# P times V of some key tiles as three f16 products: an attention and gated-linear kernel on one Trainium2 core

## The chip, the core and the metric

The kernel runs on one core of a Trainium2 chip. Its engines work in parallel, each on its own instructions and strictly in their order: PE (TensorE) multiplies matrices into PSUM, ACT (ScalarE) applies functions, DVE (VectorE) and Pool (GpSimd) work on elements, and SP (SyncE) starts the transfers (DMAs). They wait for each other by semaphores. The metric is the device time of one execution in microseconds (us). Before the change it is 1651.75 us, the median of three runs (1650.93 to 1652.77).

## The reference, cut to what matters

```python
B, S, D, H = 1, 2048, 512, 32           # 32 heads of 16, one shared key and value head; F = 1792
mod = (silu(c) @ w_mod).reshape(1, 6, 1, -1)
sa, ca, ga, sb, cb, gb = ...            # six rows of mod
h = layernorm(x) * (1 + ca) + sa
q, k, v = h @ wq, h @ wk, h @ wv        # q in 32 heads, k and v in one
p = softmax(q @ k.T * 16 ** -0.5)       # per head, 2048 x 2048
x = x + ga * ((p @ v) @ wo)             # heads side by side
h = layernorm(x) * (1 + cb) + sb
x = x + gb * (((h @ w_gate) * (h @ w_up)) @ w_down)
```

All inputs and the output are f32.

## The kernel before, in words

**Units and turns.** The attention is cut into 32 units (`u`). Unit u has the 256 queries of block `sb = u // 4` and the 8 heads of group `ch = u % 4`. The loop at L1328 goes through the units, and in each through 16 key tiles of 128 keys (`kt`). One key tile of one unit is a turn; `attend` (L1247) writes out two turns. Two points of a turn will be named often: its middle, and `end_turn` at its end.

In a turn, `qk_exp` (L652) is called four times. Each call makes scores of 128 keys by 512 columns (two heads of 256 queries) on PE and has ACT take their exponential into an f32 tile `P` of 128x512. The row maximum is already in the scores: q carries rows with the negative maximum, and 50 rows take part in the product. The maxima of the next unit are made at the same time: each turn holds four products `mx` (L605) that DVE reduces (L609). At the end of the turn, `pv` (L669) multiplies the P tiles of the turn before with the values: four f32 matmuls at L674, one for each P tile, each with the same 32 columns of `vst` (16 of v, 16 of ones, whose product is the sum of the softmax) and each writing its own 32 partitions of one PSUM bank over all 16 key tiles of the unit. So the four stand in four column strips of PE, and use all its 128 rows.

**Side work.** Between these, each turn has eight places for the other matmuls (the `x` in the string `MANY`, L62): the projection of q, the output projection `wo_work`, gate and up (`gu`), and down. They are f16 products with halves: a factor is split into a high and a low f16 half, and three products (high-high, low-high, high-low, `TERMS`) stand for the f32 one. They use 64 rows of PE each and run beside a score or maximum product on the other 64. They are taken in order from the queue `fill`; a group of gate and up takes 24 places, which is three turns. `half` (L527) makes a group that goes over from one half of the rows to the other wait for an exponential of the turn before (`sync`).

At step 20 of every fourth unit (two steps to a turn) `hooks` (L1307) puts the output projection of the block just done into `fill`, behind what runs and at most one more group, and behind it the rest, with the new block's gate, up and down at the end.

**After a group.** A finished gate and up group is evicted at the end of its turn: ACT and DVE multiply (L868, L870), Pool splits the product into the two f16 halves of `glu` (L871, L872). `glu` has two places, one for blocks with even number and one for odd.

When the second of the two output projection groups (t = 1) is evicted, L755 adds into x, and `after` (L722) puts the rest on ticks. A tick is a call of `drain_posts` (L1148), at the start and in the middle of every turn; in the middle it comes ahead of `hooks`. Counted from that eviction, the statistics come at tick 3 (L762) and tick 4 (L765, then the reciprocal root on Pool, L213 to L218), and the normalisation of the block's two row tiles, `nrm` (L771), at ticks 4 and 9 (L793). For blocks 2 to 5 all of `nrm` is on Pool: L774, L780, L781, L783, L784, each 128x512; for block 6 ACT does the first. Then SP turns the result over by a transposing DMA (L807), four ticks after `nrm`.

**The end of a unit.** The last `pv` of unit u stands at the end of turn 0 of unit u+1, and `pv_out` (L677) at the end of turn 1: ACT copies the bank with a scale `evs`, SP stores it. `normalise` (L685) then follows in four parts at steps 5, 12, 15 and 19 (`NORM_AT`): SP loads the sums and the products, DVE takes the reciprocal, SP spreads it, and Pool multiplies and splits into `och` (L710 to L713), the last of these at the end of turn 9.

SP's queue also carries, in program order, the loads of q for later units (L570) and the rows with the maximum (L643).

Of the kernel before, what the change touches and what calls it, by code (L numbers as in the profile page):

```python
# [39 lines left out]
LATE_Q = 3  # L40
NORM_AT = (5, 12, 15, 19)
NBANK = 8
# [7 lines left out]
PAIRED = 14  # L50
Q_BURSTS = {26: 3, 27: 3, 28: 3, 29: 3}

LOW = -3.0e38
# [12 lines left out]
def adaln_mqa_glu_kernel(ctx: ExitStack, tc: tile.TileContext, x_in, wq_in, wk_in, wv_in, wo_in,  # L66
# [82 lines left out]
    for i in range(3):  # L149
        t = consts.tile([128, 2, 2, ST], F16, name=f"sst{i}")  # L150
        if i == 2:
            nc.gpsimd.memset(t, 0.0)
        sst.append(t)
# [5 lines left out]
    nc.gpsimd.memset(onec, 1.0)  # L159
    ones = consts.tile([128, 128], F32, name="ones")  # L160
# [13 lines left out]
    def marks():  # L174
        lo2 = ident.rearrange("p (a r) -> p a r", a=2)
        for col, r0, r1 in ((0, 16, 32), (1, 32, 48), (2, 48, 50)):
# [122 lines left out]
    def q_evac(u, p):  # L299
        split_rows(sst[u][:, :, p, :], pks[u, p], qsc, sck[:, 3:4], 0.0)  # L300
        ps_give(pks[u, p])
# [16 lines left out]
    def v_mm(b):  # L318
        p = ps_hold("pvt", (128, 4, 16))
        for i in range(4):  # L320
            nc.tensor.matmul(p[:, i, :], parts[b][:, i * 128:(i + 1) * 128], lane[:, 16:32], start=True, stop=True)  # L321

        def out():
            nc.scalar.activation(vst[:, 4 * b:4 * b + 4, 0:16], p, AF.Copy, scale=inv[:, 0:1] if b else 1.0)
            ps_give(p)
        posts.append(out)
# [48 lines left out]
    kb = consts.tile([128, 8], F32, name="kb")  # L375
    inv = consts.tile([128, 3], F32, name="inv")
    fwd = consts.tile([128, 3], F32, name="fwd")
    nc.vector.tensor_copy(kb[:, 0:4], pb[:, 0:4])
# [23 lines left out]
    ln_norm(1, (None, nc.scalar, None, nc.scalar))  # L402
    evs = consts.tile([128, 1], F32, name="evs")

    def ev_scales():

        t = work.tile([128, 2], F32, name="evt", bufs=1)
        nc.vector.tensor_reduce(evs, ident.rearrange("p (a r) -> p a r", a=4)[:, :, 0:16], axis=AX.XY, op=OP.add)
        nc.vector.reciprocal(t[:, 0:1], kb[:, 5:6])
        nc.gpsimd.tensor_tensor(t[:, 0:1], t[:, 0:1], evs, op=OP.mult)  # L410
        nc.gpsimd.tensor_scalar(t[:, 1:2], evs, -1.0, 1.0, op0=OP.mult, op1=OP.add)
        nc.gpsimd.tensor_tensor(evs, t[:, 0:1], t[:, 1:2], op=OP.add)

    qvs = consts.tile([128, 1], F32, name="qvs")
# [42 lines left out]
    def last_rows():  # L457
        wmb = big.tile([128, KC, 1536], F32, name="wmB", tag="wu")
        nc.sync.dma_start(wmb, wm_v[:, :, 1536:3072])
        wmB.append(wmb)  # L460

    wmB = []
    KA, KB = (0, 1), (2, 3)
# [3 lines left out]
    first = {0: lambda: (combine((0, 1), selq), ln_tr(1), ln_stats(6)),  # L467
             1: lambda: (q_evac(0, 1), v_mm(0), ln_norm(2, (VE, SA, VE, SA)), ln_stats(7),
                         q_part(1, 0), q_part(1, 1)),
# [8 lines left out]
             12: lambda: (k_evac(3), h_halves(3, KA)), 13: lambda: h_halves(3, KB),  # L478
             15: lambda: h_halves(1, KA), 17: lambda: h_halves(1, KB), 20: ev_scales}
    later_h = deque((2, k) for k in range(KC))  # L480
# [4 lines left out]
    ended = []  # L485
    sync = {"due": False, "exp": None, "before": None}
    pending = []

    def flush():
        for f in pending:  # L490
            f()
            sync["due"] = True
        pending.clear()

    class Group:
# [31 lines left out]
        def half(self, r):  # L527

            mm = self.put(r, r + 1)
            if self.rows not in (None, r):  # L530
                tc.add_manual_dep(mm.ins, sync["before"], SYNC)
            self.rows, self.turn, sync["due"] = r, now[0], True
            if self.ended():
                ended.append(self)
# [114 lines left out]
    och = {}  # L649
    pd = {}  # L650

    def qk_exp(u, kt, p, a, last=False):  # L652
        s = sst[u % 3]
        ptl[u, kt, p, a] = work.tile([128, D], F32, name="P", tag="P", bufs=8)
        t = ps_sc()
        keys = kst[64 * a:64 * a + 50, kt * 128:(kt + 1) * 128]
        if pending and last:
            for c in range(2):
                if c:
                    flush()  # L660
                nc.tensor.matmul(t[:, c * ST:(c + 1) * ST], keys, s[64 * a:64 * a + 50, c, p, :], start=True, stop=True)  # L661
        else:
            nc.tensor.matmul(t.rearrange("k (c n) -> k c n", c=2), keys, s[64 * a:64 * a + 50, :, p, :],  # L663
                             start=True, stop=True)
        ex = nc.scalar.activation(ptl[u, kt, p, a], t, AF.Exp)  # L665
        if sync["due"]:
            sync.update(due=False, exp=ex.ins.name)

    def pv(u, kt):  # L669
        if kt == 0:  # L670
            pvb[u] = ps_hold("pv")
        for j in range(4):
            p, a = divmod(j, 2)
            nc.tensor.matmul(pvb[u][32 * j:32 * j + 32, :], vst[:, kt, :], ptl[u, kt, p, a],  # L674
                             start=(kt == 0), stop=(kt == KT - 1))

    def pv_out(u):  # L677
        sb, ch = divmod(u, NC)
        ev = work.tile([128, BT], F32, name="ev", tag="ev", bufs=3)
        nc.scalar.activation(ev, pvb[u], AF.Copy, scale=evs)  # L680
        ps_give(pvb[u])
        pd[u] = dram.tile([128, BT], F32, name=f"pd{u}")
        nc.sync.dma_start(pd[u], ev)
# [127 lines left out]
    def ln2_work(sb):  # L811
        st = {}

        def tr(i):
            def f():
                if not h2s:
                    h2T = big.tile([128, 2, 2, KC, ST], F16, name="h2T", tag="wq")
                    glus.append(big.tile([128, 2, 2, FT, ST], F16, name="glu", tag="big"))
# [34 lines left out]
    def ffn_work(sb):  # L853

        def glu():
            return glus[0][:, sb % 2]

# [374 lines left out]
    def side_half(r, cur=cur):  # L1232
# [11 lines left out]
        if cur[0].did[r] < cur[0].n:  # L1244
            cur[0].half(r)

    def attend(u, kt):  # L1247

# [9 lines left out]
        def end_turn(kt):  # L1258
            for g in ended:
                g.finish()  # L1260
            ended.clear()
            for f in ends:
# [12 lines left out]

        for turn in range(2):
            now[0] = u * NSTEP + 2 * (kt + turn)
            sync["before"] = sync["exp"]
            drain_posts()
# [27 lines left out]
    def hooks(u, i):  # L1307
# [4 lines left out]
        side_step(step)  # L1312
        if u > 0 and i in NORM_AT:
            if i == NORM_AT[0]:
                nrm[:] = normalise(u - 1)
            nrm[NORM_AT.index(i)]()
        if i == 20 and u > 0 and u % NC == 0:
            sb = u // NC - 1
# [23 lines left out]

    pv(u, KT - 1)
    pv_out(u)
    sync["before"] = sync["exp"]
# [60 lines left out]
```

## Time and profile before

| | |
|---|---|
| median of three runs | 1651.75 us |
| the profiled execution | 1650.64 us |
| its span, first to last instruction | 1648.9 us |
| PE busy | 1630.6 us, 99% |
| DVE busy | 1401.6 us, 85% |
| ACT busy | 1224.0 us, 74% |
| Pool busy | 554.8 us, 34% |
| clock granted to PE, mean | 0.997 |

The profile comes from one execution. Busy time is the union of an engine's instructions. Matmuls overlap, and their ends are modelled, so for PE the distance from one start to the next says more than a duration. In a line of the timeline the first number is the start in us from the span's start, the second how long the merged instructions took, then come engine, source line, operation, output and inputs, shapes and the count; a bracket tells of idle time of that engine just before, and what ended it. Line numbers are those of the kernel before.

### The profile page before, as it was taken

What the parts mean: (1) busy time and instruction counts of PE and PEld (TensorE: products, weight loads), DVE (VectorE), ACT (ScalarE), POOL (GpSimd) and SP (SyncE); (2) the same over time, 40 slices, a digit from 0 to 9 for tenths busy, and PEclk for the clock granted to TensorE, in tenths of its full rate; (3) what the DMA queues carried; (4) which work ended last, traced back from release to release, by engine and by line L of the source; (5) the groups of instructions that cost most, each with busy time, mean ns of one, the idle gap of its engine ahead of it and who ended that gap; (6) DMA issues with size and microseconds to landing.
All of it is one profiled execution on the core that took longest, in us unless ns stands there. A gap on an engine that the chain in (4) does not pass through costs nothing.

```text
span 1648.9 us, 39747 instructions
## 1 busy us (share of the span) xinstructions
PE 1630.6 (99%) x15629; PEld 743.0 (45%) x15629; DVE 1401.6 (85%) x2434; ACT 1224.0 (74%) x2365; POOL 554.8 (34%) x859
## 2 busy tenths in 40 slices
PE   8999999999999999999999999999999999999998
PEld 4333333355533554335543455434545345444776
DVE  7999999899999999999999999999999999980211
ACT  6688888888877787778877787777778777877300
POOL 5856637864842111401113011400114001410322
PEclk9999999999999999999999999999999999999999
DMA  7213313342211001100001000100001000100100
GB/s 259 97 55 101 94 54 121 91 136 81 78 50 37 20 12 31 38 26 20 20 28 35 26 17 20 39 26 26 20 28 29 26 23 20 39 15 21 33 14 13
DMA packets 78987, 79.05 MB, mean 48 GB/s; under 512 B 30408, under 2 KB 59340, under 8 KB 78800
## 3 DMA queue, kind: packets, MB, share of 16 engines
q1 hardware_dynamic: 77744, 76.46, 15.2%
q8 instruction: 122, 2.00, 0.5%
q14 instruction: 65, 0.53, 0.1%
q10 hardware_dynamic: 1056, 0.07, 0.0%
HBM read 56.04 MB, written 17.05 MB: 44 GB/s over the span
## 4 chain that ended last, share of the span: by engine, by line
PE 94%; ACT 2%; DVE 1%; DMA 1%; issue 1%; POOL 0%; ACTq 0%; SPq 0%
PE side L515 42%; PE pv L674 30%; PE mx L605 8%; PE sc L663 8%; PE sc L661 3%; ACT P L665 1%; DVE mpart L609 1%; DMA xbig<-in_A_x_dram 1%; PE part L283 0%; PE sc L605 0%; PE mxt L633 0%; PE pk L291 0%; DMA wkv<-in_A_wv_dram 0%; DMA sst<-qd 0%; PE pvt L321 0%
## 5 line engine op out<-in xcount | busy, mean ns | idle before, releaser
L609 DVE TENSOR_REDUCE mpart<-mx 128x1 f32<-128x512 f32 x2016 | 1273.9, 684 | 93.2 <-PE mx L605 86.8
L665 ACT ACTIVATE P<-sc 128x512 f32<-128x512 f32 x2048 | 1095.3, 598 | 282.6 <-PE sc L663 235.1
L605 PE MATMUL mx<-kst,sst 48*128 48x512 f16 x2032 | 629.2, 377 | 2.6 <-DMA sst<-qd 0.8
L663 PE MATMUL sc<-sst,kst 50*128 50x512 f16 x1792 | 597.8, 379 | 0.6 <-ACT P L665 0.3
L674 PE MATMUL pv<-P,vst 128*32 128x512 f32 x4096 | 545.4, 605 | 0.7
L515 PE MATMUL side<-h2T,wg 64*128 64x256 f16 (+1 forms) x2396 | 540.5, 271 | 0.2
L515 PE MATMUL side<-h2T,wu 64*128 64x256 f16 (+1 forms) x2396 | 538.2, 270 | 0.0
L515 PEld LDWEIGHTS <-wg 64*128 64x128 f16 (+1 forms) x2396 | 226.1, 94 | 234.7 <-ACT P L665 199.0
L515 PE MATMUL side<-wd,glu 64*128 64x512 f16 (+1 forms) x1172 | 271.7, 378 | 0.2 <-ACT P L665 0.2
L871 POOL TENSOR_SCALAR glu<-gf 128x256 f16<-128x256 f32 x112 | 45.9, 409 | 655.2 <-DVE gf L870 528.5
L515 PEld LDWEIGHTS <-wu 64*128 64x128 f16 (+1 forms) x2396 | 226.6, 95 | 38.0 <-issue 2.6
L605 PEld LDWEIGHTS <-sst 48*128 48x128 f16 x2064 | 189.9, 94 | 35.0 <-issue 17.4
L663 PEld LDWEIGHTS <-kst 50*128 50x128 f16 x1792 | 163.1, 94 | 62.8 <-issue 50.3
L515 PEld LDWEIGHTS <-glu 64*128 64x128 f16 (+1 forms) x1172 | 98.7, 95 | 194.1 <-ACT P L665 90.9
L674 PEld LDWEIGHTS pv<-P,vst 128*32 128x32 f32 x4096 | 80.9, 108 | 161.0 <-issue 150.1
L870 DVE TENSOR_TENSOR gf<-side,g 128x256 f32<-128x256 f32 x112 | 46.7, 417 | 79.4 <-ACT g L868 77.7
L661 PE MATMUL sc<-sst,kst 50*128 50x256 f16 x512 | 97.0, 268 | 0.0
L515 PE MATMUL side<-h,wq 64*128 64x512 f16 (+1 forms) x372 | 95.0, 376 | 0.4 <-ACT P L665 0.4
L868 ACT ACTIVATE g<-side 128x256 f32<-128x256 f32 x112 | 42.3, 379 | 65.9 <-PE side L515 65.6
L515 PE MATMUL side<-wo,och 64*128 64x512 f16 (+1 forms) x360 | 86.2, 378 | 0.0
L872 POOL TENSOR_TENSOR glu<-gf,glu 128x256 f16<-128x256 f32 x112 | 75.3, 672 | 9.3
L710 POOL TENSOR_TENSOR oc<-oc,rr 128x256 f32<-128x256 f32 x31 | 22.6, 730 | 147.8 <-PE sc L663 44.0
(239 smaller groups left out, 871.2 us busy)
## 6 DMA issues: line engine op xcount, KB each, us to landing
pd<-ev SPq DMA_DIRECT2D x32, 256.0 KB
kwb<-in_B_w_gate_dram SPq DMA_DIRECT2D x32, 224.0 KB
kwb<-in_B_w_up_dram SPq DMA_DIRECT2D x32, 224.0 KB
sst<-qd SPq DMA_DIRECT2D x180, 32.0 KB
qd<-q SPq DMA_DIRECT2D x16, 256.0 KB
oc<-pd SPq DMA_DIRECT2D x64, 64.0 KB
rr<-ri SPq DMA_DIRECT2D x64, 64.0 KB
x<-in_A_x_dram SPq DMA_DIRECT2D x14, 256.0 KB
```

The lines of the kernel that those rows point to most:

```text
L515: return nc.tensor.matmul(self.p[:, c * w:(c + 1) * w], left[rows], right[rows], start=start and c == 0, stop=stop and c == len(terms) - 1)
L605: nc.tensor.matmul(m, s[64 * a:64 * a + 48, t // 2, p, t % 2 * 128:(t % 2 + 1) * 128], w[64 * a:64 * a + 48, :], start=(i == 0), stop=(i = ...
L609: nc.vector.tensor_reduce(part, m, axis=AX.X, op=OP.max)
L661: nc.tensor.matmul(t[:, c * ST:(c + 1) * ST], keys, s[64 * a:64 * a + 50, c, p, :], start=True, stop=True)
L663: nc.tensor.matmul(t.rearrange("k (c n) -> k c n", c=2), keys, s[64 * a:64 * a + 50, :, p, :], start=True, stop=True)
L665: ex = nc.scalar.activation(ptl[u, kt, p, a], t, AF.Exp)
L674: nc.tensor.matmul(pvb[u][32 * j:32 * j + 32, :], vst[:, kt, :], ptl[u, kt, p, a], start=(kt == 0), stop=(kt == KT - 1))
L710: eng.tensor_tensor(o, o, st["r"], op=OP.mult)
L868: nc.scalar.activation(g, p[:, 0:ST], AF.Copy, scale=2.0 ** -45)
L870: nc.vector.tensor_tensor(gf, p[:, ST:2 * ST], g, op=OP.mult)
L871: nc.gpsimd.tensor_scalar(glu()[:, 0, f, :], gf, 1.0, 0.0, op0=OP.mult, op1=OP.add)
L872: nc.gpsimd.tensor_tensor(glu()[:, 1, f, :], gf, glu()[:, 0, f, :], op=OP.subtract)
```

## The change

From unit 9 on, two or three of the 16 key tiles of a unit are "split tiles": 0, 5 and 10, and in units with u % 4 = 1 only 0 and 10 (`F16_FROM`, `F16_AT`). That is 63 tiles in 23 units.

- The exponentials of a split tile go to one of two fixed sets of four places instead of the P buffers, and Pool splits each of the four P tiles into a high and a low half (`p_split`: a `tensor_scalar` and a `tensor_tensor`, 128x512 each). The calls are in the middle of a turn, behind `hooks`, one P tile in each of the four turns after the split tile's own. For tile 0 of units with u % 4 = 1 they are in turns 1, 1, 9 and 10 (`F16_LATE`).
- Their P times V are twelve f16 matmuls: three products for each of the four column strips, term by term. They stand where the next split tile would have had its four (`pv_place`); the last ones stand after the loop. For tile 0 of a unit with u % 4 = 1 that is the end of turn 11.
- So the last product of a unit now stands at the end of turn 1 of the next, and `pv_out` at the end of turn 2. `NORM_AT` counts from there: the four parts come two steps later than before from unit 10 on, and the step at which the output projection is put into `fill` is 22 instead of 20.
- In a turn that ends with such a burst, ACT gets a one-element copy ahead of the last exponential; the matmul that goes over to the other rows waits for it instead of the exponential (`early`).
- The scores get a 51st row that adds 14 ln 2, so P is larger by 2^14; the scale `evs` is gone, and its factors are in `vst` (`v_scales`). `prow` and the third query buffer's start value take some more instructions on Pool at the start of the kernel.
- The two sets of places lie in the second half of the old `glu`; `glu` has one place for all blocks.

```diff
-NORM_AT = (5, 12, 15, 19)
+NORM_AT = (2, 9, 12, 16)
+F16_FROM = 9
+F16_AT = ((0, 5, 10), (0, 10), (0, 5, 10), (0, 5, 10))
+F16_LATE = {0: (1, 1, 9, 10)}
+P_SHIFT = float(14 * np.log(2.0))
...
+    prow = consts.tile([128, 2], F32, name="prow")
+    nc.gpsimd.tensor_tensor(prow[:, 0:1], ident[:, 50:51], ident[:, 114:115], op=OP.add)
+    nc.gpsimd.tensor_scalar(prow[:, 1:2], prow[:, 0:1], -P_SHIFT / 32.0, 0.0, op0=OP.mult, op1=OP.add)
+    nc.gpsimd.tensor_scalar(prow[:, 0:1], prow[:, 0:1], P_SHIFT / 32.0, 0.0, op0=OP.mult, op1=OP.add)
+    nc.gpsimd.memset(sst[2], 0.0)
+    nc.gpsimd.tensor_scalar(sst[2], sst[2], prow[:, 1:2], 0.0, op0=OP.add, op1=OP.add)
...
+    f16s = [KT * u + k for u in range(F16_FROM, NU) for k in F16_AT[u % NC]]
+    f16_set = {v: i % 2 for i, v in enumerate(f16s)}
+    f16_before = dict(zip(f16s[1:], f16s))
+    f16_split = {}
+    for v in f16s:
+        late = v % KT == 0 and v // KT % NC == 1
+        for j in range(4):
+            f16_split.setdefault(v + (F16_LATE[0][j] if late else j + 1), []).append((v, j))
...
+        if last and sync["early"]:
+            ex = nc.scalar.activation(tok[:, 1:2], tok[:, 0:1], AF.Copy)
+            tc.add_manual_dep(ex.ins, sync["half"], SYNC)
+            sync.update(due=False, exp=ex.ins.name)
...
+    def p_split(v, j):
+        t, h = p_sets[f16_set[v]]
+        nc.gpsimd.tensor_scalar(h[:, j, 0], t[:, j], 1.0, 0.0, op0=OP.mult, op1=OP.add)
+        nc.gpsimd.tensor_tensor(h[:, j, 1], t[:, j], h[:, j, 0], op=OP.subtract)
...
-    def pv(u, kt):
-        if kt == 0:
+    def pv(v):
+        u, kt = divmod(v, KT)
+        if u not in pvb:
             pvb[u] = ps_hold("pv")
...
+        if v in f16_set:
+            h, i = p_sets[f16_set[v]][1], kts16.index(kt)
+            terms = [(v16[:, vl, i], [h[:, 2 * a + p, pl] for p, a in heads]) for vl, pl in ((0, 0), (1, 0), (0, 1))]
+        else:
+            terms = [(vst[:, kt, :], [ptl[u, kt, p, a] for p, a in heads])]
+        for n, (vt, ps) in enumerate(terms):
+            for j in range(4):
+                nc.tensor.matmul(pvb[u][32 * j:32 * j + 32, :], vt, ps[j], start=start and n == 0,
+                                 stop=stop and n == len(terms) - 1)
+        if stop:
+            ends.append(lambda: pv_out(u))
+
+    def pv_place(v):
+        return f16_before.get(v) if v in f16_set else v
...
         def glu():
-            return glus[0][:, sb % 2]
+            return glus[0]
...
-            v = u * KT + kt - 1
-            if v >= 0:
-                pv(*divmod(v, KT))
-                if v % KT == KT - 1:
-                    ends.append(lambda: pv_out(u - 1))
+            v = pv_place(u * KT + kt - 1) if u + kt else None
+            if v is not None:
+                pv(v)
...
                     hooks(u, 2 * (kt + turn))
+                    for vj in f16_split.get(u * KT + kt + turn, ()):
+                        p_split(*vj)
...
-        if u > 0 and i in NORM_AT:
-            if i == NORM_AT[0]:
+        since = i - out_at[0]
+        if u > 0 and i >= 3 and since in NORM_AT:
+            if since == NORM_AT[0]:
...
-        if i == 20 and u > 0 and u % NC == 0:
+        if since == NORM_AT[3] + 1 and i > 17 and u > 0 and u % NC == 0:
...
-    pv(u, KT - 1)
-    pv_out(u)
+    pv(KT * NU - 1)
+    pv(f16s[-1])
```

More of the change, by code (lines that the diff above doesn't have):

```diff
@@ L159, in adaln_mqa_glu_kernel @@
     nc.gpsimd.memset(onec, 1.0)
-    ones = consts.tile([128, 128], F32, name="ones")
+    ones = work.tile([128, 128], F32, name="ones", tag="n2", bufs=2)
     nc.gpsimd.memset(ones, 1.0)
     rows = consts.tile([128, 3], F32, name="rows")
+    prow = consts.tile([128, 2], F32, name="prow")
[4 more added lines that the diff above has]
+    nc.gpsimd.tensor_scalar(sst[2], sst[2], prow[:, 1:2], 0.0, op0=OP.add, op1=OP.add)
     lane = consts.tile([128, 32], F32, name="lane")
@@ L299, in q_evac @@
     def q_evac(u, p):
-        split_rows(sst[u][:, :, p, :], pks[u, p], qsc, sck[:, 3:4], 0.0)
+        split_rows(sst[u][:, :, p, :], pks[u, p], qsc, sck[:, 3:4], prow[:, 0:1])
         ps_give(pks[u, p])
@@ L323, in out @@
         def out():
-            nc.scalar.activation(vst[:, 4 * b:4 * b + 4, 0:16], p, AF.Copy, scale=inv[:, 0:1] if b else 1.0)
+            nc.scalar.activation(vst[:, 4 * b:4 * b + 4, 0:16], p, AF.Copy, scale=vsc[:, 1:2] if b else vsc[:, 0:1])
             ps_give(p)
@@ L376, in adaln_mqa_glu_kernel @@
     inv = consts.tile([128, 3], F32, name="inv")
+    vsc = consts.tile([128, 2], F32, name="vsc")
+    tok = consts.tile([1, 2], F32, name="tok")
+    nc.gpsimd.memset(tok, 0.0)
+    kts16 = sorted({k for ks in F16_AT for k in ks})
+    v16 = consts.tile([128, 2, len(kts16), 32], F16, name="v16")
     fwd = consts.tile([128, 3], F32, name="fwd")
@@ L485, in adaln_mqa_glu_kernel @@
     ended = []
-    sync = {"due": False, "exp": None, "before": None}
+    sync = {"due": False, "exp": None, "before": None, "half": None, "early": False}
     pending = []
@@ L490, in flush @@
         for f in pending:
-            f()
-            sync["due"] = True
+            sync.update(due=True, half=f().ins.name)
         pending.clear()
@@ L531, in half @@
                 tc.add_manual_dep(mm.ins, sync["before"], SYNC)
-            self.rows, self.turn, sync["due"] = r, now[0], True
+            self.rows, self.turn = r, now[0]
+            sync.update(due=True, half=mm.ins.name)
             if self.ended():
@@ L650, in adaln_mqa_glu_kernel @@
     pd = {}
+    f16s = [KT * u + k for u in range(F16_FROM, NU) for k in F16_AT[u % NC]]
+    assert f16s[0] % KT == 0
+    f16_set = {v: i % 2 for i, v in enumerate(f16s)}
[5 more added lines that the diff above has]
+            f16_split.setdefault(v + (F16_LATE[0][j] if late else j + 1), []).append((v, j))
+    p_sets = []
+    did_pv = {}
     def qk_exp(u, kt, p, a, last=False):
         s = sst[u % 3]
-        ptl[u, kt, p, a] = work.tile([128, D], F32, name="P", tag="P", bufs=8)
+        v = u * KT + kt
+        if v in f16_set:
+            ptl[u, kt, p, a] = p_sets[f16_set[v]][0][:, 2 * a + p]
+        else:
+            ptl[u, kt, p, a] = work.tile([128, D], F32, name="P", tag="P", bufs=8)
         t = ps_sc()
-        keys = kst[64 * a:64 * a + 50, kt * 128:(kt + 1) * 128]
+        keys = kst[64 * a:64 * a + 51, kt * 128:(kt + 1) * 128]
         if pending and last:
@@ L667, in qk_exp, with p_places @@
             sync.update(due=False, exp=ex.ins.name)
-    def pv(u, kt):
-        if kt == 0:
-            pvb[u] = ps_hold("pv")
[L672 to L675, printed above, removed]
+    def p_split(v, j):
+        t, h = p_sets[f16_set[v]]
+        nc.gpsimd.tensor_scalar(h[:, j, 0], t[:, j], 1.0, 0.0, op0=OP.mult, op1=OP.add)
+        nc.gpsimd.tensor_tensor(h[:, j, 1], t[:, j], h[:, j, 0], op=OP.subtract)
+    def p_places(both):
+        n = 9 * D
+        for i in range(2):
+            t = both[:, i * n:(i + 1) * n]
+            p_sets.append((t[:, D:].bitcast(F32).rearrange("p (j t) -> p j t", j=4),
+                           t[:, :8 * D].rearrange("p (j h t) -> p j h t", j=4, h=2)))
+        for i, k in enumerate(kts16):
+            nc.gpsimd.tensor_scalar(v16[:, 0, i], vst[:, k, :], 1.0, 0.0, op0=OP.mult, op1=OP.add)
+            nc.gpsimd.tensor_tensor(v16[:, 1, i], vst[:, k, :], v16[:, 0, i], op=OP.subtract)
+    def pv(v):
+        u, kt = divmod(v, KT)
+        if u not in pvb:
+            pvb[u] = ps_hold("pv")
+            did_pv[u] = 0
+        start, stop = did_pv[u] == 0, did_pv[u] == KT - 1
+        did_pv[u] += 1
+        heads = [divmod(j, 2) for j in range(4)]
+        if v in f16_set:
+            h, i = p_sets[f16_set[v]][1], kts16.index(kt)
+            terms = [(v16[:, vl, i], [h[:, 2 * a + p, pl] for p, a in heads]) for vl, pl in ((0, 0), (1, 0), (0, 1))]
+        else:
+            terms = [(vst[:, kt, :], [ptl[u, kt, p, a] for p, a in heads])]
[7 more added lines that the diff above has]
+        return f16_before.get(v) if v in f16_set else v
     def pv_out(u):
@@ L817, in f @@
                     h2T = big.tile([128, 2, 2, KC, ST], F16, name="h2T", tag="wq")
-                    glus.append(big.tile([128, 2, 2, FT, ST], F16, name="glu", tag="big"))
+                    both = big.tile([128, 2 * KC * S], F16, name="glu", tag="big")
+                    n = 2 * FT * ST
+                    glus.append(both[:, :n].rearrange("p (h f t) -> p h f t", h=2, f=FT))
+                    p_places(both[:, n:])
                     h2s.update({s: h2T[:, s % 2] for s in range(NS)})
@@ L1245, in side_half @@
             cur[0].half(r)
+    out_at = [0]
     def attend(u, kt):
@@ L1261, in end_turn @@
             ended.clear()
+            if ends:
+                out_at[0] = 2 * kt + 1
             for f in ends:
@@ L1278, in attend @@
             sync["before"] = sync["exp"]
+            sync["early"] = u * KT + kt + turn - 1 in f16_set
             drain_posts()
@@ L1312, in hooks @@
         side_step(step)
-        if u > 0 and i in NORM_AT:
-            if i == NORM_AT[0]:
+        since = i - out_at[0]
+        if u > 0 and i >= 3 and since in NORM_AT:
+            if since == NORM_AT[0]:
                 nrm[:] = normalise(u - 1)
-            nrm[NORM_AT.index(i)]()
-        if i == 20 and u > 0 and u % NC == 0:
+            nrm[NORM_AT.index(since)]()
+        if since == NORM_AT[3] + 1 and i > 17 and u > 0 and u % NC == 0:
             sb = u // NC - 1
@@ L1341, in adaln_mqa_glu_kernel @@
     u = NU - 1
-    pv(u, KT - 1)
-    pv_out(u)
+    pv(KT * NU - 1)
+    pv(f16s[-1])
+    for f in ends:
+        f()
+    ends.clear()
     sync["before"] = sync["exp"]
```

25 lines of the change are left out of this document (9 added, 16 removed).

## The prediction

> **What bounds the kernel now.** First the page's chain of work that ended last, by engine and by line:
>
> ```profile
> PE 94%; ACT 2%; DVE 1%; DMA 1%; issue 1%; POOL 0%; ACTq 0%; SPq 0%
> PE side L515 42%; PE pv L674 30%; PE mx L605 8%; PE sc L663 8%; PE sc L661 3%; ACT P L665 1%; DVE mpart L609 1%; DMA xbig<-in_A_x_dram 1%; PE part L283 0%; PE sc L605 0%; PE mxt L633 0%; PE pk L291 0%; DMA wkv<-in_A_wv_dram 0%; DMA sst<-qd 0%; PE pvt L321 0%
> ```
>
> PE carries 94% of it, and P times V alone 30%. Next, busy times by stretches: us of the stretch, then PE, PEld, DVE, ACT and Pool with their counts, the clock, the DMA share, GB/s.
>
> ```profile
> 50.00:100.00 50.00, 46.90 (x325) 14.91 (x325) 49.31 (x101) 33.95 (x68) 41.64 (x48) 0.93 0.24 75
> 900.00:1000.00 100.00, 99.89 (x1052) 48.05 (x1054) 92.03 (x156) 78.44 (x151) 11.09 (x20) 1.00 0.07 22
> ```
>
> In the steady part PE never rests, and Pool is nearly free (11 of 100 us). The first row, where PE had pauses, comes back below for its clock of 0.93. Then the timeline of PE through one turn in two answers, the second of which splits the product P times V into its halves:
>
> ```profile
> 900.12 0.38 PE L515 MATMUL side<-wd,glu 64*128 64x512 f16 x1
> ...
> 901.42 0.38 PE L515 MATMUL side<-wd,glu 64*128 64x512 f16 x1
> ...
> 901.78 0.64 PE L674 MATMUL pv<-P,vst 128*32 128x512 f32 x4
> 902.23 0.61 PE L674 MATMUL pv<-P,vst 128*32 128x512 f32 x4
> 902.78 0.39 PE L515 MATMUL side<-wd,glu 64*128 64x512 f16 x1
> ```
>
> From 900.12 to 901.42 lie six steps of f16 matmuls with 512 columns: 0.217 us each. The f32 product takes from 901.78 to 902.78, 1.00 us: each of its four matmuls is two instructions, the four column strips run at once, the second set starts 0.45 us after the first, and (1.00 - 2 x 0.45) = 0.10 us goes on changing over. One f32 instruction thus has two passes of 0.225 us, and the whole product four.
>
> **What the change takes away.** Three f16 products in place of four passes. At the pace of the side work the burst is 3 x 0.217 + 0.10 = 0.75 us, at that of the f32 passes 3 x 0.225 + 0.10 = 0.78. I take 0.76, so 0.24 saved, between the two since both are f16-speed passes of the same length: 63 tiles x 0.24 = 15.1 us (14.2 to 15.8). All 63 bursts are on PE's stream, so this is worth its full size unless a turn becomes bound by another engine. A turn with a burst lasts 2.84 - 0.24 = 2.60 us (the turn of 2.84: the rows of DVE below come every 2.84 us). What DVE and ACT need for four of theirs:
>
> ```profile
> 871.90 2.53 DVE L609 TENSOR_REDUCE mpart<-mx 128x1 f32<-128x512 f32 x4 [0.30 <-PE mx L605]
> ```
>
> ```profile
> 1072.13 2.17 ACT L665 ACTIVATE P<-sc 128x512 f32<-128x512 f32 x4 [0.48 <-PE sc L663]
> ```
>
> DVE's four take 2.53 and it then waits 0.30 for PE (2.83 together); it stays just inside 2.60. ACT's 2.17 leave 0.43 for the added one-element copy. Neither takes the bound, but DVE's slack is nearly gone in such turns; three of 16 turns have it, so it catches up in the next.
>
> **What it adds: Pool's place in the queue.** In all, Pool gets 63 x 4 splits. What one costs, and where they fall, is seen in unit 17, the first of the units with u % 4 = 1 from block 3 on. DVE fixes the turns there:
>
> ```profile
> 864.02 0.18 DVE L765 BATCH_NORM_AGGREGATE st<-bs 128x2 f32<-128x6 f32 x1
> 864.11 4.58 DVE L609 TENSOR_REDUCE mpart<-mx 128x1 f32<-128x512 f32 x7
> 868.60 0.42 DVE L870 TENSOR_TENSOR gf<-side,g 128x256 f32<-128x256 f32 x1
> ```
>
> L765 is tick 4 after the output projection. Seven reductions later a group is evicted, which happens only at a turn's end; with four to a turn, three belonged to the turn of L765, so L765 came behind the first reduction: in that turn's middle. The product P times V of turn 11 (quoted below, 875.90; found by counting the products of L674) has that of turn 9 two turns of 2.84 us ahead, at 870.2, and that of turn 8 at 867.4. So the eviction at 868.60 is that of turn 8, 1.2 us behind it, and L765 is the middle of turn 7. So `nrm` of the first row tile is issued in the middle of turn 7 (tick 4), and of the second at the start of turn 10 (tick 9). Pool, in the same stretch:
>
> ```profile
> 866.24 2.09 POOL L774 TENSOR_SCALAR n<-x,st,ry 128x512 f32<-128x512 f32 x1
> ...
> 871.12 0.62 POOL L783 TENSOR_SCALAR n<-n 128x512 f16<-128x512 f32 x1
> 871.82 1.16 POOL L784 TENSOR_TENSOR n<-n,n 128x512 f16<-128x512 f32 x1
> 872.94 0.40 POOL L871 TENSOR_SCALAR glu<-gf 128x256 f16<-128x256 f32 x1
> ...
> 874.06 0.73 POOL L710 TENSOR_TENSOR oc<-oc,rr 128x256 f32<-128x256 f32 x1
> ...
> 876.02 2.08 POOL L774 TENSOR_SCALAR n<-x,st,ry 128x512 f32<-128x512 f32 x1
> ```
>
> The order agrees: first row tile (866.24 to 872.94, 6.70 us), the evicted group (to 874.06), `och` (issued at the end of turn 9, to 876.02), second row tile (start of turn 10). Pool is behind PE here. One split is what L783 and L784 do: 871.12 to 872.94, 1.82 us.
>
> Now the change. Tile 0 of this unit is split in turns 1, 1, 9 and 10, and its burst ends turn 11. Pool's queue becomes: first row tile, group, split 3 (middle of turn 9), second row tile (start of turn 10), split 4 (middle of turn 10), `och` (now end of turn 10). So: 874.06 + 1.82 = 875.88, + 6.70 = 882.58, + 1.82 = 884.40. PE wants split 4 for the burst of turn 11. Where PE stands at these places, four answers, for units 13, 17, 25 and 29:
>
> ```profile
> 690.84 0.64 PE L674 MATMUL pv<-P,vst 128*32 128x512 f32 x4
> 875.90 0.64 PE L674 MATMUL pv<-P,vst 128*32 128x512 f32 x4
> 1246.62 0.64 PE L674 MATMUL pv<-P,vst 128*32 128x512 f32 x4
> 1431.52 0.64 PE L674 MATMUL pv<-P,vst 128*32 128x512 f32 x4
> ```
>
> Unit 17 gets there at 875.90 and would be through at 876.66. Its third product needs the low half of split 4, from 884.40, and then 0.22 + 0.10: 884.72. PE stands for 8.1 us, and behind that matmul in its queue stands everything: the scores, so ACT; the maxima, so DVE; the side work. The bursts before unit 17 move PE and Pool alike, since the row tiles start from PE's output projection.
>
> The other units, Pool:
>
> ```profile
> 685.07 1.16 POOL L784 TENSOR_TENSOR n<-n,n 128x512 f16<-128x512 f32 x1
> ...
> 1244.68 0.72 POOL L710 TENSOR_TENSOR oc<-oc,rr 128x256 f32<-128x256 f32 x1
> ...
> 1427.78 0.73 POOL L710 TENSOR_TENSOR oc<-oc,rr 128x256 f32<-128x256 f32 x1
> ...
> 1429.72 1.27 POOL L780 TENSOR_TENSOR n<-n,cbb 128x512 f32<-128x512 f32 x1
> ...
> 1434.26 0.40 POOL L871 TENSOR_SCALAR glu<-gf 128x256 f16<-128x256 f32 x1
> ```
>
> Unit 25 is like 17: 1244.68 + 10.34 + 0.32 = 1255.34 against 1246.62 + 0.76 = 1247.38, 8.0 us; unit 21, between them, has the same order, 8.0. In unit 29 ACT does part of `nrm`, and Pool's share is 1429.72 to 1434.26, 4.54: 1427.78 + 1.82 + 4.54 + 1.82 + 0.32 = 1436.28 against 1432.28, 4.0. In unit 13 the output projection had ended three turns earlier, so the second row tile is over at 686.23, two splits at 689.87, ahead of 690.84: nothing. In unit 9 `late` puts the first row tile on turn 11, behind both splits: nothing. Sum of the waits: 8.1 + 8.0 + 8.0 + 4.0 = 28.1 us.
>
> **The clock after such a wait.** The first stretch above, with PE pausing, lost 7% of the clock in 50 us, 3.5 us. No pause of 8 us stands in the steady part, so this is bounded: nothing, or 3.5 us for each wait. I take 2.5 for the three long ones and 1.0 for the short one, nearer the upper end as those waits are longer than any pause there: 8.5 us (0 to 14).
>
> The Trainium skill (TensorE: Matmul & The Clock Gate, Part 1) says the clock falls to half after an idle window of about 3.4 us and returns after a busy one. By that page each wait costs an estimated 1.7 to 3.4 us, the four 6.8 to 13.6 instead of my 8.5.
>
> **What costs nothing.** At the start Pool gets a 128x1024 addition (2 x 0.62) and three one-column ones (at most 0.24 each), 2.0 us, under this pause; without it they would delay the first normalisation by as much:
>
> ```profile
> 8.45 0.24 POOL L213 TENSOR_SCALAR rv<-st 128x4 f32<-128x4 f32 x1 [5.11 <-DVE st L254]
> ```
>
> `normalise` and its seven transfers come one turn later. On SP they pass no load that is due, and the two transposing DMAs wait for Pool's row tiles at the times of before: the first is untouched, and for the second a split has taken the place of `och` (1.82 against 874.06 to 876.02). The single `glu` is free when it is written, as down of a block is ahead of the next gate and up in PE's order. The 51st row adds no column. The other splits are called two turns and a half or more ahead of their burst, on a Pool that has 11% to do.
>
> **Sum.** 1648.9 - 15.1 + 28.1 + 8.5 = 1670.4 for the span of the profiled execution (1650.64 with what lies around it; the median is 1.1 us above that). On the median: 1651.75 + 21.5 = 1673.
>
> **Rivals.**
> *Split 4 is ready in time* (ends faster). If units 17 to 29 had their row tiles where unit 13 has them, three turns earlier, no burst would wait: 1651.75 - 15.1 = 1636.6. It decides at 876.3, when PE asks for split 4; were the second row tile merely behind split 4, it would be ready at 877.70, a wait of 1.4 us in each of three units: 1640.9. For it: the calls at 9 and 10 fit unit 13 exactly. Against it: nothing in the change moves the groups, since, counted back from unit 17 in threes, they change over in the middle of turns 9 and 12 of units 16, 20, 24 and 28, and step 20 or 22 (turn 10 or 11) meets the same one. Chance 0.15, and 0.02 for a mixture that ends level.
> *Weights are not loaded ahead.* Then each later term shows its load:
>
> ```profile
> L674 PEld LDWEIGHTS pv<-P,vst x8: 106/108/109, 901.8 to 901.8; 128*32 128x32 f32 x8
> ```
>
> Two loads of 0.108 make the burst 0.97 and the gain 63 x 0.03 = 1.9: 1651.75 - 1.9 + 28.1 + 8.5 = 1686.5. Against it: all eight loads were made at 901.8, the second four while the first matmuls ran. 0.04. This is what a rule of the Trainium skill (TensorE: Matmul & The Clock Gate, Part 3) would do, by which a load overlaps a running matmul only in another row group; here all share one, and the trace disagrees.
> *The strips don't run at once in f16.* Twelve matmuls at the pairs' rate of 0.108 are 1.30 + 0.10, 0.40 worse than now: 1651.75 + 25.2 + 28.1 + 8.5 = 1713.6. The f32 rows show four strips at once with twice the bytes. 0.03.
>
> **How the numbers follow.** The forecast has 0.76. Its own range: gain 14.2 to 15.8, clock 0 to 14, waits a tenth shorter or longer (2.8): 1661 to 1682. To leave out no more than 2 in 10 it reaches up to the second rival: 1661 to 1687. A measurement here tells about 0.2% from no change. Faster 0.15, level 0.02, slower 0.83.
>
> **What would show it.** Right: in units 17, 21, 25 and 29 a gap of PE of 4 to 8 us at the end of turn 11, ended by Pool, with L774 (or L780) between the third and fourth split; a clock below 1.00 behind it; other bursts at 0.75 to 0.78 us. Wrong: bursts that wait nowhere (1637), bursts near 1 us, waits in other units, or a DVE without its 0.30.

## The result and the profile after

The kernel after takes 1673.66 us, the median of four runs (1672.46 to 1676.41), beside 1652.26 for the kernel before in the same session (1650.93 to 1654.36). The ratio is 1.0133, with a 95% interval of 1.0121 to 1.0146: slower by 1.3%. The profiled execution took 1674.18, its span is 1672.3, 23.4 more than before. Its chain of work that ended last, by engine:

```profile
PE 86%; POOL 6%; DVE 4%; ACT 2%; issue 1%; DMA 0%; SPq 0%; POOLq 0%; ACTq 0%; DVEq 0%
```

PE carried 94% of the chain before and Pool 0%; now Pool holds 6% of it. Which wait that is, the view of waits says (us in total, how often, the longest):

```profile
PE pv L724 <- POOL glu L696: 24.1, 5, 7.0
```

L696 makes the high half of a split and L697 the low one; both read and write the sets in the old `glu`, whose name they bear here. P times V waits for a high half five times in the whole kernel, 7 us at the longest. The timeline of PE shows one of them, at the end of turn 11 of unit 17:

```profile
874.88 0.40 PE L724 MATMUL pv<-glu,v 128*32 128x512 f16 x3
882.25 1.04 PE L724 MATMUL pv<-glu,v 128*32 128x512 f16 x8 [6.97 <-POOL glu L696]
883.49 0.59 PE L724 MATMUL pv<-glu,v 128*32 128x512 f16 x1 [0.19 <-POOL glu L697]
884.00 0.60 PE L520 MATMUL side<-wd,glu 64*128 64x512 f16 x1
...
884.40 0.63 PE L520 MATMUL side<-wd,glu 64*128 64x512 f16 x1
```

Three strips of the first product run, the fourth needs the high half of the fourth P tile and comes 7 us later; the last matmul of the burst waits once more, for the low half. Behind the wait, two steps of side work start 0.40 us apart, where 0.217 is usual: about half the pace. Pool in the same stretch:

```profile
865.22 2.09 POOL L829 TENSOR_SCALAR n<-x,st,ry 128x512 f32<-128x512 f32 x1
...
871.94 0.40 POOL L929 TENSOR_SCALAR glu<-gf 128x256 f16<-128x256 f32 x1
...
873.07 0.62 POOL L696 TENSOR_SCALAR glu<-glu 128x512 f16<-128x512 f32 x1
...
874.91 2.07 POOL L829 TENSOR_SCALAR n<-x,st,ry 128x512 f32<-128x512 f32 x1
...
881.58 0.62 POOL L696 TENSOR_SCALAR glu<-glu 128x512 f16<-128x512 f32 x1
882.28 1.16 POOL L697 TENSOR_TENSOR glu<-glu 128x512 f16<-128x512 f32 x1
883.39 0.72 POOL L765 TENSOR_TENSOR oc<-oc,rr 128x256 f32<-128x256 f32 x1
```

From 865.22 on it does things in the order of its queue without a rest: first row tile, group (871.94), split 3 (873.07), second row tile (874.91), split 4 (881.58), `och` (883.39). The split that PE stands for is 1.8 us of work behind 6.7 us that nobody waits for. Elsewhere the new burst does what it is for; the same timeline of PE, a burst and an f32 product one turn later:

```profile
915.64 0.83 PE L724 MATMUL pv<-glu,v 128*32 128x512 f16 x12
916.40 0.39 PE L520 MATMUL side<-wd,glu 64*128 64x512 f16 x1
...
918.24 1.07 PE L724 MATMUL pv<-P,vst 128*32 128x512 f32 x8
919.24 0.39 PE L520 MATMUL side<-wd,glu 64*128 64x512 f16 x1
```

From the burst to the next matmul 0.76 us, from the f32 product 1.00. Last, the stretches (us, then PE, PEld, DVE, ACT and Pool, the clock, the DMA share, GB/s):

```profile
880.00:887.00 7.00, 4.56 (x25) 1.34 (x24) 1.30 (x3) 1.68 (x3) 6.58 (x9) 0.52 0.17 40
...
900.00:1000.00 100.00, 100.00 (x1073) 47.26 (x1071) 93.44 (x157) 79.96 (x161) 56.44 (x72) 1.00 0.08 25
```

In the steady part PE is full as before, and Pool has gone from 11 to 56 of 100 us. From 880 to 887, around the end of the wait, the granted clock is 0.52, about half.

### The profile page after: what moved, and what is told of

Read it like the earlier page. It is cut to its first block, busy times and chain, and to the rows that moved or that the text cites. A ratio compares the mean times of both kernels' runs of the same rounds, so it can differ in the third digit from the quotient of the medians.

```text
span 1672.3 us, 41157 instructions
## 1 busy us (share of the span) xinstructions
PE 1629.1 (97%) x15881; PEld 752.0 (45%) x15881; DVE 1401.4 (84%) x2433; ACT 1221.9 (73%) x2428; POOL 1004.5 (60%) x1372
## 3 DMA queue, kind: packets, MB, share of 16 engines
q1 hardware_dynamic: 77744, 76.46, 14.4%
## 4 chain that ended last, share of the span: by engine, by line
PE 86%; POOL 6%; DVE 4%; ACT 2%; issue 1%; DMA 0%; SPq 0%; POOLq 0%; ACTq 0%; DVEq 0%
PE side L520 39%; PE pv L724 27%; PE sc L684 8%; PE mx L611 8%; DVE mpart L615 3%; PE sc L682 3%; ACT P L690 1%; POOL n L829 1%; POOL glu L697 1%; POOL n L836 1%; POOL n L835 1%; POOL n L839 1%; PE part L291 0%; DMA wmA<-in_w_mod_dram 0%; PE mxt L639 0%
## 5 line engine op out<-in xcount | busy, mean ns | idle before, releaser
L690 ACT ACTIVATE P<-sc 128x512 f32<-128x512 f32 x1796 | 969.5, 599 | 247.7 <-PE sc L684 202.4
L684 PE MATMUL sc<-sst,kst 51*128 51x512 f16 x1792 | 601.3, 381 | 0.7 <-ACT P L690 0.3
L724 PE MATMUL pv<-P,vst 128*32 128x512 f32 x3592 | 480.1, 607 | 0.7
L697 POOL TENSOR_TENSOR glu<-glu 128x512 f16<-128x512 f32 x252 | 291.8, 1158 | 21.1
L696 POOL TENSOR_SCALAR glu<-glu 128x512 f16<-128x512 f32 x252 | 155.6, 618 | 98.0 <-ACT glu L690 67.8
L684 PEld LDWEIGHTS <-kst 51*128 51x128 f16 x1792 | 163.7, 95 | 63.9 <-issue 51.1
L690 ACT ACTIVATE glu<-sc 128x512 f32<-128x512 f32 x252 | 139.1, 596 | 60.3 <-PE sc L684 57.2
L724 PEld LDWEIGHTS pv<-P,vst 128*32 128x32 f32 x3592 | 71.1, 108 | 142.2 <-issue 132.5
L682 PE MATMUL sc<-sst,kst 51*128 51x256 f16 x512 | 97.1, 269 | 0.0
L926 ACT ACTIVATE g<-side 128x256 f32<-128x256 f32 x112 | 42.3, 379 | 66.1 <-PE side L520 65.7
```

The lines of the kernel that those rows point to most:

```text
L696: nc.gpsimd.tensor_scalar(h[:, j, 0], t[:, j], 1.0, 0.0, op0=OP.mult, op1=OP.add)
L697: nc.gpsimd.tensor_tensor(h[:, j, 1], t[:, j], h[:, j, 0], op=OP.subtract)
L724: nc.tensor.matmul(pvb[u][32 * j:32 * j + 32, :], vt, ps[j], start=start and n == 0, stop=stop and n == len(terms) - 1)
L926: nc.scalar.activation(g, p[:, 0:ST], AF.Copy, scale=2.0 ** -45)
```

## The experiments

Each is a single edit, of the kernel after or of experiment 1. Where one run is given, it is one execution with a profile, beside 1651.66 (seven runs; first four experiments) or 1651.79 (one run; last three) for the kernel before on the same chip. The theory: the burst saves 0.24 us 63 times, and the place of split 4 behind the second row tile costs more than that. To compare traces turn by turn I take the starts of the exponentials: a lost wait shifts all later ones.

**1. The splits of the late tiles without delay.** The burst stays at the end of turn 11.

```
-F16_LATE = {0: (1, 1, 9, 10)}
+F16_LATE = {0: (1, 2, 3, 4)}
```

> Tile 0 of units with u % 4 = 1 is split in turns 1 to 4 like every other; all else as changed. Theory (the waits come from one split standing behind a row tile in Pool's order): no burst waits in units 9, 17, 21, 25 and 29, and the clock stays at 1.00 from unit 9 to the end. The turns 11 and 12 of these units lost 9.5, 8.0, 9.1, 6.7 us and 1.7 us in unit 9 against before; about 36 us go, 1.1 us may come back in unit 21, where the maxima waited for the loads of q: 1673.7 - 35 = 1638 to 1640, faster than before by 0.8%. Rival (Pool has too much to do on the whole, or the bursts themselves lose the clock): 1655 or more, with waits at other bursts.

Measured: 1637.28 us, the median of four runs (1636.00 to 1637.51); ratio to before 0.9911, interval 0.9895 to 0.9928. All waits of PE for splits are gone, that of unit 9 too. In unit 17, Pool and then PE:

```profile
870.51 0.67 POOL L930 TENSOR_TENSOR glu<-gf,glu 128x256 f16<-128x256 f32 x1
871.17 2.08 POOL L829 TENSOR_SCALAR n<-x,st,ry 128x512 f32<-128x512 f32 x1
```

```profile
872.95 0.83 PE L724 MATMUL pv<-glu,v 128*32 128x512 f16 x12
873.72 0.39 PE L520 MATMUL side<-wd,glu 64*128 64x512 f16 x1
```

The second row tile follows the group, and the burst of turn 11 takes its 0.77 us. So the placement of the last splits costs 36.4 us, waits and clock together, and without it the change wins 14.4. It is also the fastest version here: faster than both kernels.

**2. Both late splits in turn 9,** the same burst, so only the order on Pool is turned.

```
-F16_LATE = {0: (1, 1, 9, 10)}
+F16_LATE = {0: (1, 1, 9, 9)}
```

> Only the last split of tile 0 moves, from turn 10 to turn 9, so that it stands ahead of the second row tile (1, 1, 9, 9). Theory (order, priced by what stands ahead): in units 17, 21 and 25 two splits of 1.82 us follow the group, the wait falls from 8 to about 1.4 us each and the clock stays up; in unit 29 nothing; in unit 9 under 0.5. About 1638.5 + 4 = 1643. Rival (the wait is set by Pool's backlog of several turns, not by what stands directly ahead): waits stay at 6 us or more, time above 1660.

Measured: 1643.95 us. Pool and PE in unit 17:

```profile
873.03 0.62 POOL L696 TENSOR_SCALAR glu<-glu 128x512 f16<-128x512 f32 x1
...
874.98 0.62 POOL L696 TENSOR_SCALAR glu<-glu 128x512 f16<-128x512 f32 x1
...
876.83 2.08 POOL L829 TENSOR_SCALAR n<-x,st,ry 128x512 f32<-128x512 f32 x1
```

```profile
874.81 0.40 PE L724 MATMUL pv<-glu,v 128*32 128x512 f16 x3
875.66 0.61 PE L724 MATMUL pv<-glu,v 128*32 128x512 f16 x8 [0.45 <-POOL glu L696]
...
877.20 0.39 PE L520 MATMUL side<-wd,glu 64*128 64x512 f16 x1
```

The burst takes 877.20 - 874.81 = 2.39 us, 1.63 more than 0.76. One step of the queue turned, and 8.2 us become 1.6. Units 17, 21 and 25 have this wait (1.5 to 1.6), unit 29 has none at turn 11. Unit 9 has none there either; the burst of its tile 10, in unit 10, now waits about 1.2, as the four splits of that tile stand behind both row tiles. So 1643.95 lies 6.7 above experiment 1, and these four waits make 5.9 of it.

**3. A fourth product in each burst,** on top of experiment 1. It adds the low-low product, which the kernel does not need.

```
-... for vl, pl in ((0, 0), (1, 0), (0, 1))]
+... for vl, pl in ((0, 0), (1, 0), (0, 1), (1, 1))]
```

> As e1_no_late, with the fourth product, low half of v times low half of P, in each of the 63 bursts (the result gets closer to f32, nothing is left out). Theory (a term is one pass of 0.217 to 0.225 us, its weights are loaded while the term before runs): 63 x 0.22 = 13.9 us over e1_no_late. Rival (each further term shows its weight load of 0.108 us): 63 x 0.33 = 20.6 us over it.

Measured: 1654.20 us, 16.9 over experiment 1, between the two values expected, so the time alone does not decide. The burst does:

```profile
850.73 0.55 PEld L724 LDWEIGHTS <-v 128*32 128x32 f16 x16 [0.43 <-issue]
850.73 1.05 PE L724 MATMUL pv<-glu,v 128*32 128x512 f16 x16
851.71 0.39 PE L520 MATMUL side<-wo,och 64*128 64x512 f16 x1
```

It takes 0.98 us, 0.22 more than three products, and turn by turn each burst costs 0.213 to 0.218: 63 x 0.216 = 13.6. The other 3.3 lie at four places: the maxima wait for loads of q in units 13, 21 and 25 (1.12, 0.72 and 0.60 more than in experiment 1), and 0.9 lies ahead of unit 9, where the edit does nothing. The first line shows the sixteen weight loads (PEld, 0.092 to 0.097 us each): they are over at 851.28, while matmuls of the burst still run, so they are hidden. A rule of the Trainium skill (TensorE: Matmul & The Clock Gate, Part 3) lets a load overlap only a matmul in another row group; these strips share all rows, and the load is hidden all the same, so the trace differs from it.

**4. PE kept busy in the wait.** The kernel after, with 30 products of no use (13 in unit 29) ahead of the burst. They change what PE does in the wait, not when the splits come.

```
+        if v % KT == 0 and u % NC == 1 and u >= 17:
+            p = ps_mx("warm")
+            for _ in range(30 if u < 29 else 13):
+                nc.tensor.matmul(p, kst[:, 0:128], kst[:, 0:512], start=True, stop=True)
```

> The kernel as changed, with PE kept busy while it waits: ahead of the burst of tile 0 in units 17, 21 and 25 stand 30 f16 matmuls of 512 columns into a bank that nobody reads, in unit 29 there are 13 (6.5 and 2.8 us; they are added work, all else is the same). Theory (the wait itself is Pool's, and behind it the clock costs 1.3 to 1.7 us in the long ones and about 2.5 in unit 29): the clock keeps 1.00 from unit 9 on, the waits themselves stay, and the time falls by 6 to 8 us to about 1667. Rival (what is lost behind the waits is the other engines starting up again): no change, or slower.

Measured: 1666.88 us, 6.8 less than after. PE in unit 17, and the stretch behind:

```profile
874.58 6.65 PE L725 MATMUL warm<-kst 128*128 128x512 f16 x30
881.16 0.40 PE L728 MATMUL pv<-glu,v 128*32 128x512 f16 x3
...
883.51 0.39 PE L520 MATMUL side<-wd,glu 64*128 64x512 f16 x1
```

```profile
880.00:900.00 20.00, 18.96 (x163) 6.05 (x165) 14.57 (x25) 12.50 (x26) 15.28 (x19) 1.00 0.07 15
```

The burst is through at 883.51, 8.17 us later than it would be without the wait (874.58 + 0.76), and the clock stays at 1.00. So work without use shortens the kernel by 7 us. From unit 9 on, what this trace has more than experiment 1 is the waits alone, and what the kernel after has more than this trace is the clock alone. The rival, that the other engines lose time in starting up again, is out: ACT stands 8.61 us in this wait too.

**5. Without the one-element copy** (on top of experiment 1): the matmul that changes rows behind a burst waits for the last exponential.

```
-        if last and sync["early"]:
+        if False:
```

> As e1_no_late, without the one-element copy on ACT: the first matmul after a burst that goes over to the other rows waits for the last exponential again. Theory (a burst is so short that this exponential now ends last): in e1_no_late a burst begins at 889.95 and PE goes on 0.75 us later, while the exponential starts about 0.15 us after the burst and takes 0.57 to 0.60, so it is ready at about the same time, and its signal and a weight load of 0.1 come behind it: 0.05 to 0.2 us in each of 63 turns, 3 to 12 us slower than e1_no_late. Rival (the copy is not needed): no difference in any turn with a burst, or 0.06 less, the ACT time of the copy.

Measured: 1639.25 us, 2.0 above experiment 1, less than the 3 to 12 expected. The burst and the matmul behind it:

```profile
889.18 0.83 PE L724 MATMUL pv<-glu,v 128*32 128x512 f16 x12
890.03 0.39 PE L520 MATMUL side<-wd,glu 64*128 64x512 f16 x1
```

0.85 us here instead of 0.76. From unit 9 on the trace loses 4.3 us, 0.05 to 0.08 at nearly every one of the 63 bursts; the stretch ahead of unit 9, which the edit does not touch, was 2.3 shorter in this trace, which hides half of it. The copy is worth its place, by little.

**6. Three split tiles in every unit** (on top of experiment 1). Tile 0 of units with u % 4 = 1 then has its burst where tile 5 is split, at the end of turn 6.

```
-F16_AT = ((0, 5, 10), (0, 10), (0, 5, 10), (0, 5, 10))
+F16_AT = ((0, 5, 10), (0, 5, 10), (0, 5, 10), (0, 5, 10))
```

> As e1_no_late, with tile 5 split in units with u % 4 = 1 too (0, 5, 10 everywhere, six bursts more, splits in the four turns after each). Theory (the same sum of Pool's queue): bursts gain 6 x 0.235 = 1.4 us, but tile 5's splits stand in turns 6 to 9 beside the row tiles, and its burst at the end of turn 11 waits: in units 17, 21, 25 Pool reaches the last low half 871.94 + 1.12 + 3 x 1.82 = 878.5 and the burst would be over at 875.6 without it, 3.2 us; about 1.3 in unit 29 and 2 in unit 13, none in unit 9; the splits of tile 10 come late by as much. 12 to 15 us of waits, up to 1.5 us each of clock: 1648 to 1656. Rival (waits come only from a split behind the second row tile): no waits, 1636.

Measured: 1656.77 us, 19.5 above experiment 1 and just over the 1648 to 1656 expected, though six more products are cheaper. Units 17, 21 and 25 lose 3.3 to 3.5 us at turn 11, waiting for tile 5 (3.2 expected), unit 29 1.5. Behind the waits of units 13, 17 and 25 the clock is at half for 3.41 us. Unit 13 waits too, at the end of turn 6 and behind the first row tile, not where it was expected. Its PE and its Pool:

```profile
675.66 0.40 PE L724 MATMUL pv<-glu,v 128*32 128x512 f16 x3
679.14 0.62 PE L724 MATMUL pv<-glu,v 128*32 128x512 f16 x8 [3.08 <-POOL glu L696]
```

```profile
671.77 2.10 POOL L829 TENSOR_SCALAR n<-x,st,ry 128x512 f32<-128x512 f32 x1
...
678.47 0.62 POOL L696 TENSOR_SCALAR glu<-glu 128x512 f16<-128x512 f32 x1
```

So the second row tile is not the only one that counts: in these units the last split of a tile, called two and a half turns ahead of its burst, comes late behind the first row tile, whether it is of tile 0 or of tile 5. Leaving out tile 5 in these units avoids that; the delay to turns 9 and 10 is what brings it back.

**7. The second row tile two steps later,** in the kernel after, so that it stands behind split 4.

```
-                        after((4, 9)[j] + late, n2f[2 * sb + j])
+                        after((4, 11)[j] + late, n2f[2 * sb + j])
```

> The kernel as changed, with splits of tile 0 in turns 1, 1, 9 and 10, but the second row tile is normalised at tick 11 instead of 9, at the start of turn 11, so it comes behind the last split. Theory (only the order on Pool counts): in units 17, 21 and 25 the two splits follow the group, waits of about 1.4 us as in e2_both_nine instead of 8, in unit 29 none, the clock stays up; unit 9 as changed, 1.8. About 1643 to 1646. Rival (something else in these turns holds the burst): 8 us each as before, 1665 or more.

Measured: 1665.44 us, on the rival's side: I expected 1643 to 1646. The trace shows why this does not decide. Pool in unit 17, then PE:

```profile
870.72 2.10 POOL L829 TENSOR_SCALAR n<-x,st,ry 128x512 f32<-128x512 f32 x1
...
877.45 0.62 POOL L696 TENSOR_SCALAR glu<-glu 128x512 f16<-128x512 f32 x1
...
879.27 0.41 POOL L929 TENSOR_SCALAR glu<-gf 128x256 f16<-128x256 f32 x1
...
880.39 0.62 POOL L696 TENSOR_SCALAR glu<-glu 128x512 f16<-128x512 f32 x1
...
886.00 2.08 POOL L829 TENSOR_SCALAR n<-x,st,ry 128x512 f32<-128x512 f32 x1
```

```profile
877.52 0.39 PE L724 MATMUL pv<-glu,v 128*32 128x512 f16 x1
...
881.07 0.61 PE L724 MATMUL pv<-glu,v 128*32 128x512 f16 x8 [2.55 <-POOL glu L696]
...
882.82 0.60 PE L520 MATMUL side<-wd,glu 64*128 64x512 f16 x1
```

The second row tile is behind split 4, as meant. But the edit also moved the side work: the first row tile now starts 6.8 us ahead of this burst (877.52 - 870.72; in the kernel after 874.88 - 865.22 = 9.7), and the evicted group falls between the two splits. So the first row tile took the place of the second as what split 4 is late for: the burst takes 882.82 - 877.52 = 5.30 us, 4.5 more than 0.76, with half the clock behind it, and units 13 and 29 wait as well. My reading of the edit failed: the step could not be moved alone. Gate and up stand in `fill` until the row tiles are done, so a later row tile can move all side work behind it; that this is what moved it here was not traced. The clean test of the order is experiment 2.

## Why the prediction came out, step by step

By the starts of the exponentials, over turns 11 and 12 of each unit named: a wait is experiment 4 less experiment 1 (in unit 17, with both against before, 7.94 + 0.23 = 8.17), the clock is the kernel after less experiment 4 (there 9.45 - 7.94 = 1.51). All in us:

| step of the sum | predicted | measured |
| --- | --- | --- |
| bursts, 63 of them | -15.1 | -14.9 |
| wait in unit 17, 21, 25, 29 | 8.1, 8.0, 8.0, 4.0 | 8.17, 8.05, 8.05, 3.98 |
| wait in unit 9 | 0 | 1.83 |
| clock behind the four waits | 2.5, 2.5, 2.5, 1.0 | 1.51, 1.31, 1.26, 2.90 |
| a load of q in unit 21 | not in it | -1.1 |
| ahead of unit 9 | 0 | 2.1 |
| sum | 21.5 | 23.2 |

The two profiled spans differ by 23.4, the two medians by 21.4, as the profiled run of before lies 1.6 under its median and that of after 0.5 over it. The line of bursts is experiment 1 against before from unit 9 on (-16.0), less the 1.1 in unit 21: there PE waited for a load of q in the trace of before, and does not in those of the changed kernels that I compared.

**Right: the burst,** 0.76 us. **Right: the waits**, where, why and how long. They could be had to 0.1 us each from the trace of before alone, since Pool's queue was written out with the durations of the rows of before, up to the point at which PE asks. Experiments 1 and 2 show the cause: with split 4 early the wait is gone, with it directly ahead of the row tile it is 1.5 to 1.6. Experiment 4 gives the length. Unit 13 has no wait, as said. DVE has kept its slack; an ordinary turn of the kernel after:

```profile
894.71 2.53 DVE L615 TENSOR_REDUCE mpart<-mx 128x1 f32<-128x512 f32 x4 [0.30 <-PE mx L611]
```

**Wrong: unit 9, "behind both splits: nothing".** That step asked only where the row tiles are. Pool and PE in this unit:

```profile
504.42 0.62 POOL L696 TENSOR_SCALAR glu<-glu 128x512 f16<-128x512 f32 x1
...
506.24 0.72 POOL L765 TENSOR_TENSOR oc<-oc,rr 128x256 f32<-128x256 f32 x1
...
508.17 0.62 POOL L696 TENSOR_SCALAR glu<-glu 128x512 f16<-128x512 f32 x1
```

```profile
507.80 0.40 PE L724 MATMUL pv<-glu,v 128*32 128x512 f16 x3
508.85 0.62 PE L724 MATMUL pv<-glu,v 128*32 128x512 f16 x8 [0.64 <-POOL glu L696]
510.08 0.38 PE L724 MATMUL pv<-glu,v 128*32 128x512 f16 x1 [0.62 <-POOL glu L697]
```

`och` (1.93 us, 506.24 to 508.17) stands between split 3 and split 4. The parts come two steps later only from unit 10 on, so `och` of unit 8 is still issued at the end of turn 9. The prediction had put it behind both splits in all units. Experiment 2, which calls split 4 ahead of this `och`, has no wait in unit 9.

**Mis-sized: the clock,** 8.5 in sum and 7.0 measured, and wrong in its parts: the short wait costs the most. The trace's record of the clock has a stretch at half at each of the four waits, of 6.83 us each: 879.9 to 886.7, 1071.0 to 1077.9, 1262.2 to 1269.0, 1453.3 to 1460.2. Two stretches of the kernel after, around the first and the last:

```profile
879.90:886.70 6.80, 4.26 (x23) 1.34 (x24) 1.00 (x2) 1.68 (x3) 6.38 (x9) 0.50 0.18 41
...
1453.00:1460.50 7.50, 6.88 (x50) 3.01 (x43) 2.58 (x4) 2.32 (x5) 7.08 (x10) 0.54 0.16 37
```

Half the clock costs only while PE works. In the first, PE stood until 882.25 and then waited for the low half; side work went on at 884.00, so (886.7 - 884.0) / 2 = 1.35 is lost, and some 0.2 in the last product of the burst. In the last, half begins at 1453.3, just after PE has resumed (1452.68); side work went on at 1454.43, and (1460.2 - 1454.43) / 2 = 2.9 is lost. So a price for each wait by its length was the wrong form: it is how much of the slow stretch falls behind the wait.

**Not in the sum: ahead of unit 9,** 2.1 us. The traces of the changed kernels differ there from that of before by 0.2 to 3.4, with no order by what was edited. Part is at the start, where clock stretches fall differently: the kernel after has one at half for 3.41 us at 125.5, in unit 1, and loses 1.5 of its 2.1 us in that unit; experiment 1 has it at 42.3. Units 5 to 8 lose 0.3 to 2.3 in each of them; whether the smaller instructions that Pool got for the halves of v do that was not tried, and stays open.

So the total is near for two reasons: the two large terms were each right to 0.3 us, and the errors (+1.8, -1.5, +2.1, -1.1) nearly cancel. The second is luck. Of the rivals, experiment 1 shows the first, split 4 in time, at its price (1637.28; 1636.6 was given), and experiment 2 its second form in its mechanism: the wait is 1.5 to 1.6 instead of 1.4 for each of three units. Its total (1643.95; 1640.9 was given) has the wait in unit 10 besides. Weights that are not loaded ahead, and strips not at once, are refuted by the 0.76 and by experiment 3.

## What to carry to other kernels

A nearly idle engine is not a free one: write out its queue in order with durations, and ask for each new instruction what stands ahead of it when the busiest engine wants its result. List every step that can stand there, in each kind of unit, the first one after a switch-over above all. Issue short work for a consumer early, ahead of long work that nobody waits for; here that alone turned 1.3% slower into 0.9% faster.

## What was not expected of the hardware

In the traces read for it, the clock changes on a grid of 3.41 us: the slow stretches lasted 3.41 or 6.83, and the fast ones between them whole multiples (184.32 is 54 of them, 211.63 is 62). A pause of 3.1 us in experiment 6 gave 3.41 us at half, one of 2.8 in unit 29 of the kernel after gave 6.83. In experiment 6 PE rests 2.11 us in unit 25 and 2.12 in unit 21; the first is followed by 3.41 us at half, the second by none. So a pause shorter than a step of the grid can be enough, and its length alone does not decide; that its place in the grid does is my reading. The Trainium skill (TensorE: Matmul & The Clock Gate, Part 1) has such windows of about 3.4 us; the traces agree with their length.

An f16 product over four column strips adds 0.216 us to a burst (experiment 3), the pace of one side matmul, with its four weight loads hidden.
